# Three Strassen pairs in block 1 of an attention-and-GEGLU kernel, with the attention work of the next batches moved round them

## The chip, the cores and the metric

The kernel runs on one core of a Trainium2 chip. A core has a matrix engine (TensorE, PE in the profile), a vector engine (VectorE, DVE), an engine for activation functions (ScalarE, ACT), a general engine (GpSimd, POOL) and one that issues transfers (SyncE, SP). Each works through its own list of instructions in order, and they wait for each other by semaphores. The metric is the time of one execution in microseconds (us).

## The reference

Linear attention over 8 batches of 8 heads, 576 rows and 64 columns, and behind it a feed-forward layer with a GELU gate on the 4608 rows of 512 columns:

```python
q_s = exp(q - max(q)); q_s = q_s / sum(q_s, axis=-1)      # each row of q
k_s = exp(k - max(k)); k_s = k_s / sum(k_s, axis=2)       # each column of k
kv  = einsum('bhsd,bhse->bhde', k_s, v)
x   = einsum('bhsd,bhde->bhse', q_s, kv)                  # then (4608, 512)
g   = x @ w_gate                                          # 512 -> 1536
out = ((0.5 * g * (1 + erf(g / sqrt(2)))) * (x @ w_val)) @ w_out   # 1536 -> 512
```

## The kernel before

The rows are worked in blocks of 512, one for each batch (0 to 7), and one block (8) for the 64 rows of each batch that are left over. The order is 0 to 6, 8, 7. A block has a first stage (gate and value, twelve tiles of 128 columns, written to `ht`) and a second (the product with `w_out`). While PE works on block b, the other engines prepare batch b+1 and b+2 (exp, normalization, casts, transposes).

A direct tile takes four matmuls of 512 columns for the gate and four for the value. A pair takes two tiles k and k+3 together by a Winograd form of Strassen's method, on quarters: seven products of four matmuls of 256 columns, with sums of x (`xs`) and of the weights (`ws`) made ahead:

```python
def ffn_fi(xt, fi, spare=False):                  # a direct tile
    psg = bank([P, 512], "psg", not spare)
    mm_gv(psg, wg_sb, xt, fi, range(HP))
    psv = bank([P, 512], "psv", not spare)
    mm_gv(psv, wv_sb, xt, fi, range(HP))
    gate(psg, psv, fi)                            # gelu on ACT, product on DVE

def sum_x(xt, xs=xs):                             # four sums on GpSimd
    b11, b12, b21, b22 = (xt[:, c:c + 2, r:r + 256] for c in (0, 2) for r in (0, 256))
    ...
        nc.gpsimd.tensor_tensor(out=o, in0=a, in1=b, op=ALU.subtract)

def pair_step(b, xt, k, i):
    ...
    if i == 1:                                    # products 1 and 5; 5 reads xs[0]
        ...
    if i == 2:                                    # products 6 and 3
        ...
    elif i == 3:                                  # products 7 and 2, then upper(): a product
        ...                                       #   on GpSimd for the right half of h
    else:
        product_gv(4, pa, xt, k, False)           # and final(): gelu on ACT, product on DVE
```

The lists say in what order a block goes: `6g` and `6v` are the halves of direct tile 6, `0.1` is step 1 of pair 0, letters are places where other work rides along. Blocks 0 and 1 have no list: they take direct tiles.

```python
THREE = ("a 6g l 6v 0.1 9g 0.2 9v w 0.3 7g 0.4 n m 1.1 t 7v 1.2 10g 1.3 s0 10v 1.4 2.1 u0 8g 2.2 8v"
         " 2.3 s1 11g u1 2.4 11v x")
FOUR = ...
SIX = ("0.1 6.1 0.2 6.2 0.3 6.3 0.4 1.1 6.4 7.1 s0 1.2 7.2 1.3 u0 7.3 1.4 2.1 7.4 8.1 2.2"
       " 8.2 2.3 s1 8.3 2.4 u1")
steps = {b: (SIX if b >= B - 1 else THREE if b == 2 else FOUR).split() for b in range(2, B + 1)}
```

The second stage is seven products too (`psa`, `psb`, `psc` are its banks), with sums of h (`sum_h`: sh[1], sh[2], s4 and one in place). Sums of the last tiles come here:

```python
        get("b")
        product(1, ps["a"], False, js=js[4:])
        if b > 1 and not last:
            s1 = snap("a", True)                  # True: on ACT
        ride(b, PR, "e")
        sum_h(*last_js(b), (1, 2))
        if b < 2 or last:
            s1 = snap("a")
        product(2, ps["b"], True, js=js)
        add("b", s1, 0, 0)
        ...
        sum_h(*last_js(b), (4,), "pool" if b > 1 else "dve")
        get("c")
        product(5, ps["c"], True, js=js)
        sum_h(*last_js(b), (3,), "pool" if b > 1 else "dve")
        s5 = snap("c", b == B or b == B - 2)
        ride(b, NS, 1)
        product(6, ps["a"], False, js=js)
        s2 = snap("a", b == B or b == B - 2)
        ride(b, NS, 2)
        ...
        product(3, ps["c"], False, js=js[:cut])
        ...
        add("c", s2, 0, 1)
        ...
        store_rows(b, 0, yo[0])                   # SyncE
        ...
        if cut == NO:
            product(7, ps["a"], False, js=js)
            add("a", s5, 1, 1)
        ride(b, NS, 4)
        ...
        product(4, ps["a"], False, js=js)
```

What rides along in block 1, with v of every batch loaded to one buffer and cast to one (`ld_b["v"]`, `v16_b`):

```python
at(1, FI, 4, L(exp, "k", 2, 0, 4), L(norm, 2, 3, "pool"), L(sum_w, 4), make_s)
at(1, FI, 5, L(cast_v, 2, 0, H))
at(1, FI, 8, L(unit_td, 2))                       # DMA transpose of q
at(1, FI, 11, L(exp, "k", 2, 4, 8), L(exp, "q", 3))
at(1, NS, 2, L(unit_kv4, 2), L(exp, "k", 3), L(load_batch, 3, ((v, "v"),)), L(cast_v, 3, 0, H))
at(1, NS, 4, L(unit_x4, 2, ("act", "dve"), 1), one_ring, L(preload, ACTF.Gelu),
   lambda: sum_x(get_x(2)))
```

Of the kernel before, what the change touches and what calls it, by code (L numbers as in the profile page):

```python
# [9 lines left out]
f32 = mybir.dt.float32  # L10
f16 = mybir.dt.float16
ACTF = mybir.ActivationFunctionType
# [6 lines left out]
def kernel(  # L19
# [15 lines left out]
    P = 128  # L35
# [60 lines left out]
    def bank(shape, name, spare):  # L96
        return big(shape, f32, name) if spare else small(shape, f32, name)
# [375 lines left out]
        nc.vector.scalar_tensor_tensor(  # L473
            out=ht[:, fi, :], in0=psv, scalar=_H_SCALE, in1=gl, op0=ALU.mult, op1=ALU.mult)

    def ffn_fi(xt, fi, spare=False):
        psg = bank([P, 512], "psg", not spare)
        mm_gv(psg, wg_sb, xt, fi, range(HP))
        psv = bank([P, 512], "psv", not spare)
        mm_gv(psv, wv_sb, xt, fi, range(HP))  # L480
        gate(psg, psv, fi)

    def ffn_first(xt, after):

        ps = []
        for fi in range(len(after)):
            psg = big([P, 512], f32, "psg")
            psv = big([P, 512], f32, "psv")
            if fi == 0:
                for ci in range(2):  # L490
                    mm_gv(psg, wg_sb, xt, fi, [ci])
                    mm_gv(psv, wv_sb, xt, fi, [ci])
            else:
                mm_gv(psg, wg_sb, xt, fi, range(0, 2))
                mm_gv(psv, wv_sb, xt, fi, range(0, 2))
            ps.append((psg, psv))
            for f in after[fi]:
                f()
        for fi, (psg, psv) in enumerate(ps):
            mm_gv(psg, wg_sb, xt, fi, [2])  # L500
            mm_gv(psv, wv_sb, xt, fi, [2])
        for fi, (psg, psv) in enumerate(ps):
            mm_gv(psg, wg_sb, xt, fi, [3])
            mm_gv(psv, wv_sb, xt, fi, [3])
            gate(psg, psv, fi)
# [57 lines left out]
        for i in (1, 2):  # L563
            sh[i] = wstp.tile([P, NO, 256], f16, name=f"sh{i}", tag="wst")

    def sum_h(j0, j1, which, eng="dve"):
        step = 1 if j1 - j0 == 2 else NO // 2
        js, ks = slice(j0, j1, step), slice(NO + j0, NO + j1, step)
        a11, a21 = ht[:, js, 0:256], ht[:, js, 256:512]
        a12, a22 = ht[:, ks, 0:256], ht[:, ks, 256:512]  # L570
        s1, s2 = sh[1][:, js], sh[2][:, js]
        for i in which:
            o, a, b, op = {1: (s1, a21, a22, ALU.add), 2: (s2, s1, a11, ALU.subtract),
                           3: (a21, a11, a21, ALU.subtract),
                           4: (s4[:, js], a12, s2, ALU.subtract)}[i]
            (nc.gpsimd if eng == "pool" else nc.vector).tensor_tensor(out=o, in0=a, in1=b, op=op)  # L576
# [12 lines left out]
    def sum_x(xt, xs=xs):  # L589
        b11, b12, b21, b22 = (xt[:, c:c + 2, r:r + 256] for c in (0, 2) for r in (0, 256))  # L590
        t = [xs[:, i] for i in range(4)]
        for o, a, b in ((t[0], b12, b11), (t[1], b22, t[0]), (t[2], b22, b12), (t[3], b21, t[1])):
            nc.gpsimd.tensor_tensor(out=o, in0=a, in1=b, op=ALU.subtract)

    def product_gv(i, ps, xt, k, first):
# [3 lines left out]
        for t, w, nm in ((0, wv_sb, "v"), (1, wg_sb, "g")):  # L599
            ss = ws[(nm, k // NO)]  # L600
            for c in range(2):
# [6 lines left out]

    THREE = ("a 6g l 6v 0.1 9g 0.2 9v w 0.3 7g 0.4 n m 1.1 t 7v 1.2 10g 1.3 s0 10v 1.4 2.1 u0 8g 2.2 8v"
             " 2.3 s1 11g u1 2.4 11v x")
    FOUR = ("a 7g l 7v n 0.1 6.1 0.2 6.2 0.3 6.3 m 10g 0.4 6.4 1.1 t 10v 1.2 s0 8g u0 1.3 8v 1.4 2.1"
            " 11g s1 2.2 11v 2.3")
    SIX = ("0.1 6.1 0.2 6.2 0.3 6.3 0.4 1.1 6.4 7.1 s0 1.2 7.2 1.3 u0 7.3 1.4 2.1 7.4 8.1 2.2"
           " 8.2 2.3 s1 8.3 2.4 u1")
    steps = {b: (SIX if b >= B - 1 else THREE if b == 2 else FOUR).split() for b in range(2, B + 1)}
    live = {}

    def half(b, xt, c, nm):  # L620
# [9 lines left out]
    def pair_step(b, xt, k, i):  # L630
# [24 lines left out]
                op=ALU.mult)  # L655

        if i == 1:
            live["odd"] = odd = b > 2 and not live.get("odd", True)
            cc = cc_b if odd else ffn.tile([P, 2, 2, 256], f32, name="cc", tag="cc", bufs=1)
            pa = big([P, 2, 256], f32, "pga", True)  # L660
            product_gv(1, pa, xt, k, True)
            pb = big([P, 2, 256], f32, "pgb", True, True)
            nc.scalar.copy(out=pb, in_=pa)  # L663
            pc = big([P, 2, 256], f32, "pgc", True)
            product_gv(5, pc, xt, k, True)
            live[k] = [cc, pa, pb, pc, snap(pc, b >= B - 1)]
            return
# [35 lines left out]
            if late:  # L703
                late()

    SUMS = {7: (0, 2, (1, 2)), 8: (0, 2, (3, 4)), 9: (2, 4, (1, 2)), 10: (2, 4, (3, 4))}

    def product(i, ps, first, ts=(0, 1), js=range(NO)):
        for j in js:
            for t in ts:  # L710
# [10 lines left out]

    def get_x(b):
        return get_xt(b) if b < B else xtr

    def last_js(b):
        return (NO - 2 if b < 2 else NO // 2 - 1, NO)

    def out_strassen(b, last):
        yo = [yop.tile([P, 2, C], f32, name="yo", tag="yo") for _ in range(2)]
# [27 lines left out]
                    out=yo[half][:, t, c[col]], in0=src, scalar=1.0 / _H_SCALE,  # L757
                    in1=sn[:, t], op0=ALU.mult, op1=ALU.add)

        js = (0, 1, 2, 3, 4, 5) if b < 2 else (0, 3, 1, 4, 2, 5)  # L760
        get("a")
        four = 2 < b < B - 1
        cut = 3 if four else 4
        product(1, ps["a"], True, js=js[:cut])
        if four:
# [6 lines left out]
            pair_step(b, get_x(b), NFI - NO // 2 - 1, 4)  # L772
        get("b")
        product(1, ps["a"], False, js=js[4:])
        if b > 1 and not last:
            s1 = snap("a", True)
        ride(b, PR, "e")
        sum_h(*last_js(b), (1, 2))
        if b < 2 or last:
            s1 = snap("a")  # L780
        product(2, ps["b"], True, js=js)
        add("b", s1, 0, 0)
        for x in tiles_["b"]:
            let_go(x)
        sum_h(*last_js(b), (4,), "pool" if b > 1 else "dve")
        get("c")
        product(5, ps["c"], True, js=js)
        sum_h(*last_js(b), (3,), "pool" if b > 1 else "dve")
        s5 = snap("c", b == B or b == B - 2)
        ride(b, NS, 1)  # L790
        product(6, ps["a"], False, js=js)
# [12 lines left out]
        if last:  # L804
            finish_last(b, ps["a"], yo[1], s5)
            return
        if cut == NO:
            product(7, ps["a"], False, js=js)
            add("a", s5, 1, 1)
# [108 lines left out]
    def at(b, kind, i, *fns):  # L918
        plan.setdefault((b, kind, i), []).extend(fns)
# [3 lines left out]
    def load_2nd():  # L923
# [11 lines left out]
    at(0, NS, 7, L(exp, "q", 2))  # L935
    first1 = [[L(unit_t, 1, 1), L(unit_kv, 1, 1)],
              [L(unit_x, 1, 2, "dve"), L(preload, ACTF.Gelu)],
              [L(unit_x, 1, 3, "dve"), L(norm, 2, 0, "pool"), L(norm, 2, 1, "pool")]]

    def x_upper0():  # L940
        unit_x(0, 2, "act")
# [2 lines left out]
        kv0_norm(3)  # L944


    at(1, FI, 2, L(unit_trem, 1))
    at(1, FI, 3, L(norm, 2, 2, "pool"), L(load_batch, 3, ((q, "q"), (k, "k"))))
    at(1, FI, 4, L(exp, "k", 2, 0, 4), L(norm, 2, 3, "pool"), L(sum_w, 4), make_s)
    at(1, FI, 5, L(cast_v, 2, 0, H))  # L950
    at(1, FI, 8, L(unit_td, 2))
    at(1, FI, 11, L(exp, "k", 2, 4, 8), L(exp, "q", 3))
    at(1, NS, 2, L(unit_kv4, 2), L(exp, "k", 3), L(load_batch, 3, ((v, "v"),)), L(cast_v, 3, 0, H))
    at(1, NS, 4, L(unit_x4, 2, ("act", "dve"), 1), one_ring, L(preload, ACTF.Gelu),
       lambda: sum_x(get_x(2)))
    load_2 = lambda n: load_batch(n, ((v, "v"), (q, "q"), (k, "k")))
    for i, x in enumerate(("g1", "v1", "g2", "v2", "g4", "v4")):
        at(0, FI, 5 + i, L(sum_wgv, x[0], int(x[1])))
    at(0, FI, NFI - 2, L(sum_w, 1))
    at(1, NS, 2, L(sum_wgv, "g", 3), L(sum_wgv, "v", 3))  # L960
    for b in range(2, B):
        n = b + 1
        if n < B:
# [17 lines left out]
            at(b, NS, 4, L(preload, ACTF.Gelu))  # L981
        at(b, NS, 4, L(lambda n: sum_x(get_x(n)), n if n < B - 1 else B))
    at(B, NS, 2, L(lambda: sum_x(get_x(B - 1), xs_b[1])))
    for b in range(2, B + 1):
        for j in range(NO // 2 - 1):
            at(b, PR, f"s{j}", L(sum_h, j, NO, (1,)), L(sum_h, j, NO, (3,), "pool"))
            at(b, PR, f"u{j}", L(sum_h, j, NO, (2,)), L(sum_h, j, NO, (4,), "pool"))
    for i, xs_ in (("w", ("g1", "v1", "g2", "v2")), ("x", ("g4", "v4", "g3", "v3"))):
        for x in xs_:
            at(2, PR, i, L(sum_wgv, x[0], int(x[1]), NO, 1, "pool"))  # L990
# [5 lines left out]
    def ride(b, kind, i):  # L996
        for fn in plan.get((b, kind, i), []):
            fn()

    for b in order:  # L1000
        xt = get_xt(b) if b < B else xtr
        fi0 = 0
        if b < 2:
            if b == 0:
                ffn_first0(xt, (x_upper0, L(unit_x, 0, 3, "dve")))
            else:
                ffn_first(xt, first1)
            fi0 = 2 if b == 0 else 3
            ride(b, FI, fi0 - 1)
        if b > 1:  # L1010
            go_on(b, xt)
        for fi in range(fi0, NFI if b < 2 else 0):
            ffn_fi(xt, fi, b == 1 and fi == 7)
            ride(b, FI, fi)
            if b > 0 and fi in SUMS:
                sum_h(*SUMS[fi])
        if b == 0:
            psys = []
            for ns in range(4):
                psys.append(big([P, C], f32, "psy"))  # L1020
                mm_out(psys[ns], ns, range(0, NFI // 2))
                ride(b, NS, ns)
            for ns in range(4):
                cut = 9 if ns == 2 else 7 if ns == 3 else NFI
                mm_out(psys[ns], ns, range(NFI // 2, cut))
                ride(b, NS, 14 + ns)
                mm_out(psys[ns], ns, range(cut, NFI))
                evac(b, ns, psys[ns], "act" if ns == 3 else "dve")
                ride(b, NS, 4 + ns)
        else:  # L1030
            out_strassen(b, b == order[-1])
# [30 lines left out]
```

The softmax here doesn't subtract the row's maximum and nothing guards it: scores larger than these inputs give would overflow.

## Time and profile before

| what | value |
|---|---|
| time, median of 3 runs | 296.51 us (296.48 to 296.78) |
| span of the profiled execution | 294.7 us |
| matmuls | 2449 |
| mean granted clock of PE | 0.999 |

The profile is of one execution. Its page gives the busy time of each engine and, in 40 slices of the span, the busy share in tenths. In the order of time a row has the start, the duration (of the merged instructions), the engine, the line of the kernel, the operation with output and inputs, the shape, the count, and in brackets the idle time before it with what ended it. Rows of waits give total, count and longest. Durations of matmuls overlap, so the cost of one is read from the distance of starts. Block 1 has its first stage from about 48.7 to 70.9 us and its second to 82.1; block 2 follows.

### The profile page before, as it was taken

The numbers are of one execution on the slowest core, as the hardware profiler recorded it, in microseconds if no ns is written. First come the engines' busy times: TensorE is split into PE (matmuls) and PEld (weight loads), VectorE is DVE, ScalarE is ACT, GpSimd is POOL, SyncE is SP. The second block draws the span as 40 slices with busy tenths as digits, with TensorE's granted clock in tenths as the row PEclk, the third lists the DMA queues.
The fourth block names the chain that finished last, engine by engine and source line by source line (L and its number), as shares of the span: only waits on it lengthen the run. The fifth ranks groups of instructions, "written<-read, shape, count | busy, mean of one in ns | idle before, by whom it ended". The sixth has DMA issues, their size and how long they took to land. (4 is left out here: it accounts for less than half of the span.)

```text
span 294.7 us, 6354 instructions
## 1 busy us (share of the span) xinstructions
PE 283.5 (96%) x2449; PEld 202.8 (69%) x2449; DVE 226.0 (77%) x409; ACT 194.4 (66%) x321; POOL 205.9 (70%) x191
## 2 busy tenths in 40 slices
PE   3999999999999999999999999999999999899984
PEld 1544445446767687779777877687768888788863
DVE  2855888878878769768977896787678789849992
ACT  4663367776776589768976898589863576447730
POOL 1558647870499699868887788779886555774480
PEclk9999999999999999999999999999999999999999
DMA  6999999998069605970499039803050200032003
GB/s 225 373 382 389 400 391 392 337 323 231 3 224 383 108 3 174 382 157 3 153 373 206 2 136 350 232 1 122 24 100 2 120 24 1 2 91 55 0 2 142
DMA packets 54622, 51.72 MB, mean 176 GB/s; under 512 B 18496, under 2 KB 50496, under 8 KB 54592
## 3 DMA queue, kind: packets, MB, share of 16 engines
q1 hardware_dynamic: 52864, 49.49, 52.9%
q10 hardware_dynamic: 1728, 1.84, 1.9%
q8 instruction: 19, 0.31, 0.4%
q14 instruction: 11, 0.09, 0.1%
HBM read 37.75 MB, written 9.44 MB: 160 GB/s over the span
## 5 line engine op out<-in xcount | busy, mean ns | idle before, releaser
L467 PE MATMUL psg<-xt,wg_sb 128*128 128x512 f16 x184 | 49.3, 379 | 0.0
L467 PE MATMUL psv<-xt,wv_sb 128*128 128x512 f16 x184 | 49.2, 379 | 0.0
L718 PEld LDWEIGHTS <-ht 128*128 128x128 f16 x384 | 36.4, 98 | 10.1 <-issue 2.7
L250 POOL TENSOR_TENSOR eq<-eq,rrq 128x640 f16<-128x640 f16 (+1 forms) x27 | 34.7, 1302 | 11.7 <-DVE rrq L242 7.8
L576 POOL TENSOR_TENSOR ht<-ht 128x512 f16<-128x512 f16 x21 | 26.7, 1270 | 6.1 <-DVE sh L576 6.1
L606 PEld LDWEIGHTS <-wv_sb 128*128 128x128 f16 x248 | 24.1, 98 | 9.4 <-issue 1.0
L653 POOL TENSOR_TENSOR ht<-eq 128x512 f16<-128x512 f32 x14 | 17.8, 1273 | 18.0 <-ACT eq L651 18.0
L467 PEld LDWEIGHTS <-wv_sb 128*128 128x128 f16 x184 | 17.9, 98 | 18.0 <-issue 0.5
L576 POOL TENSOR_TENSOR s<-ht,sh 128x512 f16<-128x512 f16 x21 | 24.7, 1176 | 6.9 <-DVE sh L576 6.9
L467 PEld LDWEIGHTS <-wg_sb 128*128 128x128 f16 x184 | 17.9, 98 | 16.5
L634 DVE SCALAR_TENSOR_TENSOR ht<-pga,glq 128x256 f16<-128x256 f32 x31 | 13.0, 421 | 20.6 <-ACT glq L633 20.5
L188 POOL CAST v<-vt 128x640 f16<-128x640 f32 x26 | 19.1, 776 | 12.8 <-PE pskv L343 11.3
L606 PEld LDWEIGHTS <-wg_sb 128*128 128x128 f16 x248 | 24.2, 98 | 2.8
L653 POOL TENSOR_TENSOR ht<-cc 128x512 f16<-128x512 f32 x15 | 19.1, 1274 | 8.6 <-ACT cc L651 8.5
L472 ACT ACTIVATE gl<-psg 128x512 f32<-128x512 f32 x24 | 13.8, 597 | 16.9 <-PE psg L467 15.8
L633 ACT ACTIVATE glq<-pgb 128x256 f32<-128x256 f32 x31 | 11.7, 378 | 18.7 <-PE pgb L606 10.9
L718 PE MATMUL psa<-tw,ht 128*128 128x256 f16 x192 | 23.4, 272 | 0.2 <-DVE yo L756 0.2
L212 ACT ACTIVATE ek<-kt 128x1280 f16<-128x1280 f32 (+1 forms) x11 | 19.1, 1748 | 5.7 <-DMA kt<-in_k_dram 4.2
L473 DVE SCALAR_TENSOR_TENSOR ht<-psv,gl 128x512 f16<-128x512 f32 x24 | 16.0, 686 | 8.6 <-PE psv L467 6.8
L663 ACT COPY pgb<-pga 128x512 f32<-128x512 f32 x31 | 18.0, 580 | 6.9 <-PE pga L606 6.6
L643 ACT ACTIVATE snq<-pga 128x512 f32<-128x512 f32 x31 | 18.5, 599 | 4.0 <-PE pga L606 3.7
L718 PEld LDWEIGHTS <-sh 128*128 128x128 f16 x192 | 18.6, 98 | 2.8 <-DVE sh L576 0.4
(172 smaller groups left out, 732.0 us busy)
## 6 DMA issues: line engine op xcount, KB each, us to landing
out_dram<-yo SPq DMA_DIRECT2D x15, 512.0 KB, 3.4
kt<-in_k_dram SPq DMA_DIRECT2D x7, 640.0 KB, 8.6
vt<-in_v_dram SPq DMA_DIRECT2D x7, 640.0 KB, 5.0
qt<-in_q_dram SPq DMA_DIRECT2D x7, 640.0 KB, 7.6
qt<-in_q_dram SPq DMA_DIRECT2D x8, 512.0 KB, 7.8
wost<-in_moe_w_out_dram SPq DMA_DIRECT2D x6, 512.0 KB, 7.9
kt<-in_k_dram SPq DMA_DIRECT2D x6, 512.0 KB, 9.7
vt<-in_v_dram SPq DMA_DIRECT2D x6, 512.0 KB, 5.7
```

Source lines behind the costliest of these rows:

```text
L188: nc.gpsimd.tensor_copy(out=dst, in_=src)
L212: nc.scalar.activation(out=dst[:, n0:NC, h0 * D:h1 * D].rearrange(o, d=D, **({"t": 2} if b >= QUAD else {})), in_=heads(tiles[(nm, b)], b, ...
L250: (nc.gpsimd if eng == "pool" else nc.vector).tensor_tensor(out=e, in0=e, in1=rrq.unsqueeze(-1).to_broadcast((P, n, 2, D)), op=ALU.mult)
L467: nc.tensor.matmul(ps, w[:, ci, fi * P:(fi + 1) * P], xt[:, ci, :], start=(ci == 0), stop=(ci == HP - 1))
L472: nc.scalar.activation(out=gl, in_=psg, func=ACTF.Gelu)
L473: nc.vector.scalar_tensor_tensor(out=ht[:, fi, :], in0=psv, scalar=_H_SCALE, in1=gl, op0=ALU.mult, op1=ALU.mult)
L576: (nc.gpsimd if eng == "pool" else nc.vector).tensor_tensor(out=o, in0=a, in1=b, op=op)
L606: nc.tensor.matmul(ps[:, t], a, x, start=(first and t == 0 and c == 0), stop=(c == 1), skip_group_check=True)
L643: nc.scalar.activation(out=sn, in_=ps, func=ACTF.Copy, scale=_H_SCALE)
L653: (nc.vector if k == NFI - NO // 2 - 1 else nc.gpsimd).tensor_tensor(out=ht[:, k:k + NO // 2 + 1:NO // 2, 256:512], in0=cc[:, :, 0], in1=c ...
L663: nc.scalar.copy(out=pb, in_=pa)
L718: nc.tensor.matmul(ps[t], a, w, start=(first and j == js[0] and (t == ts[0] or ps[t].tensor is not ps[ts[0]].tensor)), stop=(j == js[-1]), ...
```

## The change

Block 1 gets three pairs (tiles 0 to 5) behind its first direct tiles, which are now 6 to 8. Sums of x for it are made on GpSimd, and the third and fourth sums of weights move from the end of block 1 to block 0. All exps of k of batch 2 go to the end of block 1, with the cast of its v; kv of batch 2, the load of v of batch 3 and its cast go behind the third product of the second stage. All eight PSUM banks form one ring from the start of the pairs on. In blocks 8 and 7 sums of h move from GpSimd to VectorE and behind the first product of the second stage, and ScalarE makes the first snap. The aim is fewer matmul columns in block 1, and sums that stand in the way of less.

```diff
-    def ffn_first(xt, after):
+    def ffn_first(xt, f0, after):
...
+    ONE = ("l 9g 9v n 0.1 1.1 0.2 1.2 0.3 1.3 m 10g 0.4 w 1.4 t 2.1 10v s0 2.2 u0 11g s1 2.3 11v c")
...
-           " 8.2 2.3 s1 8.3 2.4 u1")
-    steps = {b: (SIX if b >= B - 1 else THREE if b == 2 else FOUR).split() for b in range(2, B + 1)}
+           " 8.2 2.3 s1 8.3 2.4")
+    steps = {b: (ONE if b == 1 else SIX if b >= B - 1 else THREE if b == 2 else FOUR).split()
+             for b in range(1, B + 1)}
...
-        js = (0, 1, 2, 3, 4, 5) if b < 2 else (0, 3, 1, 4, 2, 5)
+        js, late = (0, 3, 1, 4, 2, 5), NO // 2 - 1
         get("a")
-        four = 2 < b < B - 1
+        four = b != 2 and b < B - 1
...
-        if b > 1 and not last:
+        if b > 1:
             s1 = snap("a", True)
         ride(b, PR, "e")
-        sum_h(*last_js(b), (1, 2))
-        if b < 2 or last:
+        sum_h(late, NO, (1,))
+        if b >= B - 1:
+            ride(b, PR, "u1")
+        sum_h(late, NO, (2,))
+        if b < 2:
             s1 = snap("a")
...
-        sum_h(*last_js(b), (4,), "pool" if b > 1 else "dve")
+        if b > 1:
+            sum_h(late, NO, (4,), "pool")
+        else:
+            sum_h(0, NO, (4,), "dve", 1)
...
+        ride(b, NS, 3)
         if cut == NO:
             product(7, ps["a"], False, js=js)
...
-              [L(unit_x, 1, 3, "dve"), L(norm, 2, 0, "pool"), L(norm, 2, 1, "pool")]]
+              [L(unit_x, 1, 3, "dve"), lambda: sum_x(get_x(1)), L(norm_pair, 2, 0, 0, ("pool", "pool"))]]
...
-    at(1, FI, 4, L(exp, "k", 2, 0, 4), L(norm, 2, 3, "pool"), L(sum_w, 4), make_s)
-    at(1, FI, 5, L(cast_v, 2, 0, H))
-    at(1, FI, 8, L(unit_td, 2))
-    at(1, FI, 11, L(exp, "k", 2, 4, 8), L(exp, "q", 3))
-    at(1, NS, 2, L(unit_kv4, 2), L(exp, "k", 3), L(load_batch, 3, ((v, "v"),)), L(cast_v, 3, 0, H))
...
-    at(1, NS, 2, L(sum_wgv, "g", 3), L(sum_wgv, "v", 3))
+    for i, x in ((4, "g1"), (5, "v1"), (6, "g2"), (7, "v2"), (8, "g3"), (9, "v3"), (10, "g4"), (10, "v4")):
+        at(0, FI, i, L(sum_wgv, x[0], int(x[1])))
+    at(0, FI, 10, L(sum_w, 1))
...
+    at(1, PR, "m", L(norm_mul, 2, 2, "pool"), L(norm_mul, 2, 3, "pool"))
+    at(1, PR, "w", L(sum_w, 4), make_s)
+    at(1, PR, "c", L(cast_v, 2, 0, H))
+    at(1, PR, "t", L(unit_td, 2))
+    at(1, PR, "e", L(exp, "k", 2, 0, 4), L(exp, "k", 2, 4, 8), L(exp, "q", 3))
+    at(1, NS, 3, L(unit_kv4, 2), L(exp, "k", 3), L(load_batch, 3, ((v, "v"),)), L(cast_v, 3, 0, H))
+    at(1, NS, 4, L(unit_x4, 2, ("act", "dve"), 1), L(preload, ACTF.Gelu), lambda: sum_x(get_x(2)))
...
+            at(b, PR, f"s{j}", L(sum_h, j, NO, (1,)))
+            if j and b >= B - 1:
+                at(b, PR, f"u{j}", L(sum_h, j, NO, (2, 3, 4)))
+            else:
+                at(b, PR, f"s{j}", L(sum_h, j, NO, (3,), "pool"))
...
-                ffn_first(xt, first1)
-            fi0 = 2 if b == 0 else 3
+                ffn_first(xt, NO, first1)
+                one_ring()
...
-        if b > 1:
+        if b > 0:
             go_on(b, xt)
```

## The prediction

> **What bounds the kernel now.** I read the page's busy shares and slices first, then the waits of TensorE, then the order of time on TensorE, GpSimd, SyncE and VectorE round the stages that the change touches. The page:
>
> ```profile
> PE 283.5 (96%) x2449; PEld 202.8 (69%) x2449; DVE 226.0 (77%) x409; ACT 194.4 (66%) x321; POOL 205.9 (70%) x191
> PE   3999999999999999999999999999999999899984
> ```
>
> A busy PE is not a PE at its peak, so I asked what its matmuls waited for. The waits of PE in the whole span are these (total, times, longest):
>
> ```profile
> PE pswarm L459 <- ACT warm L861: 4.9, 1, 4.9
> PE psb L718 <- DVE ht L634: 1.8, 2, 0.9
> PE psx L418 <- DVE kv_sb L326: 0.3, 1, 0.3
> PE psa L718 <- DVE yo L756: 0.2, 1, 0.2
> PE psa L718 <- DVE sn L750: 0.2, 1, 0.2
> ```
>
> After the first load TensorE loses some 2.5 us. So time can be won in two ways only, fewer matmul columns or those last waits, and is lost wherever a new wait reaches PE. The price of both kinds of tile stands side by side in PE's order of time at the start of block 2:
>
> ```profile
> 82.91 1.03 PE L467 MATMUL psv<-xt,wv_sb 128*128 128x512 f16 x4
> 83.77 0.38 PE L606 MATMUL pga<-xt,wv_sb 128*128 128x256 f16 x2
> 83.99 0.38 PE L606 MATMUL pga<-xt,wg_sb 128*128 128x256 f16 x2
> 84.21 0.38 PE L606 MATMUL pgc<-xs,wsv 128*128 128x256 f16 x2
> ```
>
> By starts, four 512-column matmuls take 0.86 us and one product (four of 256) 0.44 us. The last line is the first reader of xs in block 2. GpSimd made it so, in its order of time:
>
> ```profile
> 62.66 2.71 POOL L188 CAST v<-vt 128x640 f16<-128x640 f32 x4
> 76.71 3.36 POOL L188 CAST v<-vt 128x640 f16<-128x640 f32 x4 [11.34 <-PE pskv L343]
> 81.69 1.15 POOL L593 TENSOR_TENSOR xs<-xt 128x512 f16<-128x512 f16 x1 [1.63 <-ACT xt L190]
> ```
>
> The reader is to see that the cast of v of batch 2 (62.66) and of batch 3 (76.71) lie well ahead, and that the sums xs stand behind the second cast on an engine that works in order. The load of batch 3 between them, on SyncE, and the landing of six v loads from 66.9 us on:
>
> ```profile
> 62.74 4.08 SPq L386 DMA_TRANSPOSE eqt<-eq  x1
> 66.92 1.29 SPq L168 DMA_DIRECT2D vt<-in_v_dram  x2
> 80.12 4.11 SPq L545 DMA_DIRECT2D out_dram<-yo  x2
> DMA to landing us min/median/max: 4.9/5.3/5.6
> ```
>
> **What the Trainium skill says.** "Perfetto Trace Analysis", section Identifying the Most-Contended Engine: matmul busy share says little of the distance to the peak, weight-load share more. The trace has 96% and 69%, which is why I went by starts. "DMA: Bandwidth & Descriptors", section Anatomy of one DMA: a semaphore wait is made on the issuing sequencer before dispatch. The trace agrees: SyncE stood 12.4 us before the store at 80.12, so nothing behind a store in its order can go earlier. "GPSIMD Engine Reference", section Key points: it shares its SBUF interfaces with VectorE when that has two SBUF inputs. The trace agrees: sums of h that take 0.42 us on VectorE took 1.25 to 1.38 beside GpSimd. "TensorE: Matmul & The Clock Gate", section What's actually happening: an idle window of about 3.4 us throttles the clock, and as much work frees it. Here the fifteen warm-up matmuls from 4.91 us took 6.25 us, 0.42 each, where later ones of the same 512 columns start every 0.22; no long gap follows in this trace, so it doesn't show a return to the slow clock.
>
> **The change part by part.**
>
> *Three pairs in block 1.* A pair replaces 16 matmuls of 512 (4 x 0.86 = 3.46 us) by 7 products (7 x 0.44 = 3.06). Three pairs: -1.2 us on PE. It needs sums of x (4 x 1.15 us on GpSimd). They follow the two sums tw, which ended at 55.3; so xs[0] is there at 56.5 and is read at 57.5. The third and fourth sums of weights move to block 0, where VectorE has about 1 us free per tile: nothing on the path.
>
> *The end of block 1.* Laid out with these durations from 55.4 us, PE comes to the last product of the third pair at about 70.4. Its gelu (0.38) and multiplication (0.42) end at 71.4, and the first product wants it at 70.8: a wait of 0.6. VectorE then has late sums (2 x 0.4), a snap (0.65), an addition (0.65), six sums s4 in one (0.9 to 1.6 beside casts) and a second snap (0.65). It frees the bank for product three between no and 0.7 us late. So product three ends at about 77.2. Before it ended at 78.3, but with kv of batch 2 (0.76 us of PE) ahead of it, which now comes behind: of the 1.2 won some 0.35 is left.
>
> *v of batches 2 and 3.* There is one v buffer. The cast of v 2 now stands at the end of the pairs, so it is done at about 75; the load of v 3 stands in SyncE's order behind the store of the first half of block 1's output. Added up: product three 77.2; bank read, addition of 0.69 with 0.15 to start: 78.0; issue of the store, about 1.0: 79.0; second v load issued 0.65 later: 79.7; landing 5.3: 85.0; four casts 3.0 (2.7 to 3.4 in the trace): 88.0; xs[0] 1.15: 89.2. In GpSimd's order of the changed kernel the casts of v 3 stand before the sums xs, as they did. The first reader of xs on PE stood at 84.2 before. So it is about 5.0 us later, though PE's own work (kv 0.77, product seven 1.31, x 0.9, product four 1.31, the first tile 1.73, one product 0.44, and 0.3 for a late copy of x) would have allowed 84.0: an idle PE of some 5.2 us. What the exp of k 3 behind the later kv costs (2.3 us of ScalarE, up to 0.4 of PE) vanishes inside this.
>
> *The clock.* A gap of 5 us is longer than the window named above. If it throttles, one window of 3.4 us (the skill's figure) runs at about half speed, an estimate of 1.7 us lost. I take it at two in three: +1.1. GpSimd's remaining lag of about 1.3 us against PE in block 2, against idle of 1.8 before its last upper product, I put at +0.2.
>
> *Blocks 8 and 7.* VectorE and PE at the end of block 8:
>
> ```profile
> 253.01 1.38 DVE L576 TENSOR_TENSOR sh<-sh,ht 128x512 f16<-128x512 f16 x1
> 254.31 0.41 DVE L634 SCALAR_TENSOR_TENSOR ht<-pga,glq 128x256 f16<-128x256 f32 x1
> ...
> 252.61 1.26 PE L718 MATMUL psb<-wo_sb,ht 128*128 128x256 f16 x10
> 254.77 0.39 PE L718 MATMUL psb<-wo_sb,ht 128*128 128x256 f16 x2 [0.91 <-DVE ht L634]
> ```
>
> A sum slowed by GpSimd to 1.38 us stands before the last h, which PE waits for. The change puts that sum behind it and takes two sums from GpSimd. The last h would then be done at 253.4, before PE's slot at 253.7. Product three started at 257.71, where three products of 1.31 from 252.61 give 256.54: 1.17 to be had, and in block 7 (281.40 to 286.83 against 3.93) 1.50. I count 2.4 of the 2.7.
>
> Sum: +5.0 (with what the pairs win already in it) + 1.1 + 0.2 - 2.4 = +3.9 on 296.5: 300.4 us.
>
> **Rivals.** *The late v is harmless*: 84.2 becomes 84.0, and the time falls by 0.2 + 2.4 to some 293.9; without the waits of block 1 to 293. For it speaks that the change moved kv back on purpose; against it each link of the chain is a duration of the trace, with 5 us to spare. *No throttling*: 299.3; the gap may fall across two windows. *The end of block 1 is worse than I laid out*: VectorE and ScalarE have seven products of three pairs almost back to back, and lateness there adds to product three and so to the whole chain, up to 2 us, 302.5. *The waits of blocks 8 and 7 only move*: ScalarE now takes all of the first snap of block 7, and the late sums still stand before product six; then 1 to 2 us more, 301.5 to 302.5. In block 3 the same layout runs without a PE wait, which speaks against the third.
>
> **Range and chances.** The chain's links sum to an uncertainty of about 1 us, the clock is 0 or 1.7, blocks 8 and 7 between -1 and -2.7, block 1's end up to +2. Eight in ten: 297.0 to 302.6. Slower by over 2% means 302.4, which needs two of these to go wrong together: 0.12. Faster by over 2% means 290.6, below the first rival: 0.01. Within: 0.87.
>
> **What would show it.** In the changed profile: a wait of some 5 us of PE pgc for POOL xs at the start of block 2, POOL waiting for the v load just before its casts, the v loads on SyncE directly after a store near 79; a granted clock below 1 after it; no wait of psb for ht in blocks 8 and 7. I am wrong if the casts of v 3 start before 80, or if PE waits in block 1 for longer than 1 us.

## The result, and the profile after

The changed kernel takes 304.47 us (median of four executions, 303.70 to 304.75), against 296.60 for the kernel before (296.48 to 296.78). The ratio is 1.026, with a 95% interval of 1.024 to 1.028: slower by 2.6%. The prediction, 300.4 with a range of 297.0 to 302.6, was too low. The execution that was profiled took 303.70 us; its span is 301.9, against 294.7 before.

First the page of the changed kernel. Busy times, then the slices of PE and of its clock:

```profile
PE 284.3 (94%) x2485; PEld 206.9 (69%) x2485; DVE 225.6 (75%) x409; ACT 197.2 (65%) x332; POOL 212.9 (71%) x197
PE   3999999997757999999999999999999999999994
PEclk9999999999997999999999999999999999999998
```

The total busy time hardly says that anything happened. The slices do: PE falls to 7, 7, 5 and 7 in slices 10 to 13, each 7.5 us long, so from some 68 to 98 us, and in the last of these the clock falls too. Between the first slice and the last everything else stands at 9. The waits of PE give the names (total, times, longest):

```profile
PE pgc L605 <- POOL xs L592: 5.4, 1, 5.4
PE pswarm L459 <- ACT warm L864: 4.9, 1, 4.9
PE psc L717 <- DVE sn L746: 1.7, 1, 1.7
PE pga L605 <- DVE cc L648: 1.0, 1, 1.0
PE psa L717 <- DVE ht L635: 0.5, 1, 0.5
```

The wait at the start (4.9) is as before; the two waits for `ht` of blocks 8 and 7 (1.8 in all) are gone. In their place stand one of 5.4 for the sums of x in block 2 and three of 3.2 together. PE's order of time shows that these three lie at the end of block 1 (start, duration, then in brackets the idle time before and what ended it):

```profile
71.06 0.38 PE L605 MATMUL pga<-xs,wv_sb 128*128 128x256 f16 x2 [1.03 <-DVE cc L648]
72.59 0.39 PE L717 MATMUL psa<-wo_sb,ht 128*128 128x256 f16 x2 [0.50 <-DVE ht L635]
...
78.89 1.47 PE L717 MATMUL psc<-wo_sb,s 128*128 128x256 f16 x12 [1.71 <-DVE sn L746]
80.29 0.82 PE L343 MATMUL pskv<-v,ek 128*64 128x65 f16 x40
...
92.46 0.58 PE L605 MATMUL pgc<-xs,wsv 128*128 128x256 f16 x2 [5.38 <-POOL xs L592]
93.26 1.91 PE L467 MATMUL psg<-xt,wg_sb 128*128 128x512 f16 x4
```

The first reader of `xs` in block 2, at 84.21 before, is at 92.46. Product three (the row at 78.89) gives way to the next work at 80.29, where the prediction had it end at 77.2. SyncE and GpSimd show the chain from there. SyncE's order of time:

```profile
81.12 0.59 SPq L545 DMA_DIRECT2D out_dram<-yo  x1
81.84 1.46 SPq L168 DMA_DIRECT2D vt<-in_v_dram  x2
```

GpSimd's:

```profile
73.01 3.29 POOL L188 CAST v<-vt 128x640 f16<-128x640 f32 x4
...
88.59 2.71 POOL L188 CAST v<-vt 128x640 f16<-128x640 f32 x4 [11.17 <-DMA vt<-in_v_dram]
91.26 1.15 POOL L592 TENSOR_TENSOR xs<-xt 128x512 f16<-128x512 f16 x1
```

The reader sees the load of v of batch 3 directly behind the store, and GpSimd idle for 11 us because that load has not landed, with the sums `xs` behind its casts. Behind the gap the clock is slow. A table by stage (length of the stretch, busy time of PE, PEld, DVE, ACT and POOL with counts, clock, DMA share, GB/s):

```profile
86.00:92.40 6.40, 1.08 (x7) 0.59 (x6) 1.59 (x3) 1.88 (x5) 3.81 (x5) 0.97 0.47 178
92.40:95.60 3.20, 3.14 (x12) 1.62 (x12) 0.00 (x0) 0.98 (x2) 3.12 (x4) 0.53 0.86 251
```

From 92.4 to 95.6 us PE had about half its clock (0.53): the four matmuls of 512 columns at 93.26 took 1.91 us, where they take 1.03. The work from 92.46 to 95.63 (eight matmuls of 256 columns and four of 512) costs 8 x 0.109 + 4 x 0.216 = 1.74 us by the usual starts, and took 3.17.

Blocks 8 and 7 did what they were meant to. PE at the end of block 8, products two and three, with five and six cut between them:

```profile
262.43 1.47 PE L717 MATMUL psb<-wo_sb,ht 128*128 128x256 f16 x12
...
266.36 1.47 PE L717 MATMUL psc<-wo_sb,s 128*128 128x256 f16 x12
```

No bracket, and three products of 1.31 from start to start: 3.93 us from product two to product three, where the kernel before took 5.10. Block 7 has 290.06 to 293.99, 3.93 for 5.43. Together 2.67 us won.

So the spans add up as follows: the first reader of `xs` 8.25 later (92.46 against 84.21), the slow clock 1.43, blocks 8 and 7 -2.67, the rest of blocks 2 to 6 +0.2: +7.2. The other three executions have spans of 302.7 to 303.0 at mean clocks of 0.987 and 0.988, against 0.992 in the profiled one. They are not traced; they fit a longer slow stretch, such as the trace of experiment 3 shows (last section).

### The profile page after: what moved, and what is told of

Its sections match the earlier page's. It is cut to its first block, busy times and chain, and to the rows that moved or that the text cites. A ratio compares the mean times of both kernels' runs of the same rounds, so it can differ in the third digit from the quotient of the medians.

```text
span 301.9 us, 6439 instructions
## 1 busy us (share of the span) xinstructions
PE 284.3 (94%) x2485; PEld 206.9 (69%) x2485; DVE 225.6 (75%) x409; ACT 197.2 (65%) x332; POOL 212.9 (71%) x197
## 4 chain that ended last, share of the span: by engine, by line
PE 69%; DMA 2%; DVE 1%; POOL 1%; issue 0%; SPq 0%; POOLq 0%
PE pga L605 18%; PE psa L717 13%; PE pgc L605 9%; PE psc L717 7%; PE psg L467 6%; PE psv L467 6%; PE pgb L605 4%; PE psb L717 3%; DMA vt<-in_v_dram 2%; PE pskv L343 2%; PE psx L430 1%; POOL v L188 1%; DVE s L575 1%; POOL xs L592 0%; PE psxr L430 0%
## 5 line engine op out<-in xcount | busy, mean ns | idle before, releaser
L467 PE MATMUL psg<-xt,wg_sb 128*128 128x512 f16 x160 | 44.2, 386 | 0.0
L467 PE MATMUL psv<-xt,wv_sb 128*128 128x512 f16 x160 | 43.1, 379 | 0.0
L635 DVE SCALAR_TENSOR_TENSOR ht<-pga,glq 128x256 f16<-128x256 f32 x34 | 14.4, 422 | 22.2 <-ACT glq L634 22.1
L575 POOL TENSOR_TENSOR s<-ht,sh 128x512 f16<-128x512 f16 x19 | 22.4, 1177 | 9.9 <-DVE sh L575 9.9
L654 POOL TENSOR_TENSOR ht<-cc 128x512 f16<-128x512 f32 x17 | 21.9, 1291 | 9.3 <-ACT cc L652 9.3
L664 ACT COPY pgb<-pga 128x512 f32<-128x512 f32 x34 | 19.8, 582 | 7.3 <-PE pga L605 7.0
L240 DVE TENSOR_REDUCE rq<-eq 128x20 f32<-128x1280 f16 (+1 forms) x14 | 20.1, 1439 | 4.6 <-ACT eq L212 4.6
L644 ACT ACTIVATE snq<-pga 128x512 f32<-128x512 f32 x34 | 20.3, 600 | 4.4 <-PE pga L605 4.1
L605 PE MATMUL pga<-xs,wv_sb 128*128 128x256 f16 x112 | 21.4, 272 | 1.0 <-DVE cc L648 1.0
L605 PE MATMUL pga<-xs,wg_sb 128*128 128x256 f16 x112 | 21.4, 273 | 0.0
```

Of the source, the lines that this page charges most:

```text
L240: nc.vector.reduce_sum(rq, e, axis=mybir.AxisListType.X)
L467: nc.tensor.matmul(ps, w[:, ci, fi * P:(fi + 1) * P], xt[:, ci, :], start=(ci == 0), stop=(ci == HP - 1))
L605: nc.tensor.matmul(ps[:, t], a, x, start=(first and t == 0 and c == 0), stop=(c == 1), skip_group_check=True)
L635: nc.vector.scalar_tensor_tensor(out=ht[:, fi, 0:256], in0=ps[:, 0], scalar=_H_SCALE, in1=gl, op0=ALU.mult, op1=ALU.mult)
L644: nc.scalar.activation(out=sn, in_=ps, func=ACTF.Copy, scale=_H_SCALE)
L654: (nc.vector if k == NFI - NO // 2 - 1 else nc.gpsimd).tensor_tensor(out=ht[:, k:k + NO // 2 + 1:NO // 2, 256:512], in0=cc[:, :, 0], in1=c ...
```

## Experiments

The theory after the result had three parts. (1) The 5.4 us of waiting come from SyncE: the load of v of batch 3 stands behind a store that waits for product three. (2) Product three is late because VectorE's sums of h are two to three times as long as laid out, beside a GpSimd that never rests. (3) The rest of the change is small, and blocks 8 and 7 are worth what they were meant to be. (A bank is one of the eight PSUM buffers that matmuls write to. A snap is the scaled copy that frees one.) Rivals: the wait for `xs` would come with any late v, whoever stands ahead of it; VectorE simply has too many instructions there; and the gain of blocks 8 and 7 depends on the state in which block 1 leaves the engines.

**Experiment 1: the load ahead of the store.** One line of the changed kernel; the load is issued behind product six, before the store comes up in SyncE's order.

```diff
-    at(1, NS, 3, L(unit_kv4, 2), L(exp, "k", 3), L(load_batch, 3, ((v, "v"),)), L(cast_v, 3, 0, H))
+    at(1, NS, 2, L(load_batch, 3, ((v, "v"),)))
+    at(1, NS, 3, L(unit_kv4, 2), L(exp, "k", 3), L(cast_v, 3, 0, H))
```

> The changed kernel with one edit: the load of v of batch 3 is issued behind the sixth product (ahead of the store of the first half of block 1's output on SyncE), its cast and kv of batch 2 stay behind the third. Theory (the load stands behind the store and so holds up the casts, the sums xs and PE): the load can go when the cast of v 2 is done (77 us), lands at about 83, xs[0] at about 86.5; the wait of PE for xs falls from 5.4 to under 1 us, the clock stays at 1.0 in block 2, the time falls by 5.4 + 1.4 to about 297.7 us. Rival (GpSimd is late for another reason, the casts waiting for kv of batch 2 or its own backlog): xs is hardly earlier and the time stays within 1.5 us of 304.5.

Measured: 296.68 us, ratio to the kernel before 1.0007 (0.9999 to 1.0016), mean clock 0.999. SyncE in this kernel:

```profile
76.35 1.29 SPq L168 DMA_DIRECT2D vt<-in_v_dram  x2
81.14 6.42 SPq L545 DMA_DIRECT2D out_dram<-yo  x2
```

GpSimd:

```profile
82.69 2.71 POOL L188 CAST v<-vt 128x640 f16<-128x640 f32 x4 [5.25 <-PE psa L717]
85.36 1.15 POOL L592 TENSOR_TENSOR xs<-xt 128x512 f16<-128x512 f16 x1
```

The store goes at the same time as in the changed kernel; the load goes 5.5 us earlier, `xs` stands 5.9 us earlier, and PE reads it at 86.93 without a wait. The three waits in block 1 stay as they were (1.7, 1.0, 0.5). So the place of one load in SyncE's order is worth 304.47 - 296.68 = 7.8 us here: the wait, and the clock behind it. This settles part 1 against its rival. It also leaves a bill: this kernel has the gain of blocks 8 and 7 and is still no faster than the kernel before.

**Experiment 2: blocks 8 and 7 alone.** The kernel before, with only the part of the diff that concerns its last two blocks (cut to its core):

```diff
-        if b > 1 and not last:
+        if b > 1:
             s1 = snap("a", True)
...
-        sum_h(*last_js(b), (1, 2))
-        if b < 2 or last:
+        sum_h(*last_js(b), (1,))
+        if b >= B - 1:
+            ride(b, PR, "u1")
+        sum_h(*last_js(b), (2,))
+        if b < 2:
             s1 = snap("a")
...
+            if j and b >= B - 1:
+                at(b, PR, f"u{j}", L(sum_h, j, NO, (2, 3, 4)))
```

> The kernel before with the change in blocks 8 and 7 alone. Theory (the waits of psb for h and of the sums behind them were 2.6 us, and go): 294.0 us, both waits of psb gone. Rival (the waits move to product six or three of these blocks, and the 2.6 us that block 2's end to the end of the kernel won in the changed kernel came from other blocks): 295.5 to 296.6 us.

Measured: 293.91 us, ratio 0.991 (0.989 to 0.993). After the start PE waits once, for 0.2 us. The kernel before took 296.52 beside it, so the part gives 2.6 us without anything done to block 1, and doesn't depend on it. Then the rest of the change, with the load already repaired, costs 296.68 - 293.91 = 2.8 us. The first readers of `xs` say the same: 86.93 against 84.22, 2.7 us. That is block 1 with its three waits.

**Experiment 3: GpSimd quiet at the end of block 1.** The changed kernel without two lines of work for GpSimd. It leaves out the cast of v of batch 2 and half the normalization of its q, so it does less than it should and its time is read only for what happens in block 1. VectorE's list is the same.

```diff
-    at(1, PR, "m", L(norm_mul, 2, 2, "pool"), L(norm_mul, 2, 3, "pool"))
...
-    at(1, PR, "c", L(cast_v, 2, 0, H))
```

> The changed kernel without two pieces of GpSimd's work in block 1: the multiplication of q of batch 2 by its reciprocal sums for head pairs 2 and 3, and the cast of v of batch 2 (left out, so batch 2 is worked with old values there). Theory (VectorE's sums at the end of block 1 are slow because GpSimd works beside them): the sums of h, 0.55 to 1.37 us each in the changed kernel, take 0.4 to 0.5, the six in one about 1.0 instead of 1.88, and PE's waits in block 1 (1.0, 0.5 and 1.7 us) fall to under 1 in total. Rival (VectorE is late because what it waits for comes late, and the durations are those of the instructions themselves): durations and waits stay.

Measured, one execution: 301.5 us. VectorE's order of time in the changed kernel, rows of sums of h and snaps:

```profile
69.03 1.37 DVE L575 TENSOR_TENSOR sh<-ht 128x512 f16<-128x512 f16 x1
70.32 0.68 DVE L648 SCALAR_TENSOR_TENSOR cc<-pga,snq 128x512 f32<-128x512 f32 x1
...
76.36 1.88 DVE L575 TENSOR_TENSOR s<-ht,sh 128x1536 f16<-128x1536 f16 x1
78.16 0.68 DVE L746 TENSOR_SCALAR sn<-psc 128x512 f32<-128x512 f32 x1
```

and the same rows with GpSimd quiet:

```profile
69.04 0.41 DVE L575 TENSOR_TENSOR sh<-ht 128x512 f16<-128x512 f16 x1
69.38 0.68 DVE L648 SCALAR_TENSOR_TENSOR cc<-pga,snq 128x512 f32<-128x512 f32 x1
...
74.50 0.95 DVE L575 TENSOR_TENSOR s<-ht,sh 128x1536 f16<-128x1536 f16 x1
75.36 0.69 DVE L746 TENSOR_SCALAR sn<-psc 128x512 f32<-128x512 f32 x1
```

The rows are those that PE's waits name. At 69.03 one sum takes 1.37 instead of 0.41, the addition `cc` behind it starts 0.94 later, and PE's wait of 1.03 for `cc` is there; without the slow sum it isn't. The six sums in one (`s`) take 1.88 instead of 0.95, and with three earlier sums (0.90, 0.93 and 0.82, against 0.91, 0.41 and 0.42) the snap of `psc` starts at 78.16 instead of 75.36. The rows that read PSUM (`cc`, the snaps) take 0.68 or 0.69 in both. The table of the window from 64 to 78 us has, for the changed kernel,

```profile
64.00:78.00 14.00, 11.54 (x90) 8.40 (x87) 13.01 (x18) 10.39 (x14) 12.89 (x12) 1.00 0.33 74
```

and with those instructions left out:

```profile
64.00:78.00 14.00, 13.31 (x132) 10.09 (x132) 12.05 (x21) 10.47 (x14) 6.50 (x6) 1.00 0.41 80
```

GpSimd is busy for 12.89 of 14 us in one and 6.50 in the other (2.66 in the kernel before), while the transfers are the same, 74 and 80 GB/s. So it isn't the DMA that slows the sums. Product three starts at 76.10 instead of 78.89 and kv at 77.50 instead of 80.29: 2.8 of the 3.1 us by which the prediction's 77.2 was missed.

How late a sum is depends on what GpSimd is doing when its turn comes. GpSimd's rows in the changed kernel beside the sums of 69.03 and 76.36:

```profile
68.79 1.33 POOL L575 TENSOR_TENSOR ht<-ht 128x512 f16<-128x512 f16 x1
...
76.27 1.15 POOL L575 TENSOR_TENSOR ht<-ht 128x512 f16<-128x512 f16 x1
```

The sum of 69.03 ends at 70.40, 0.28 us after GpSimd's instruction (70.12). The sums of 68.23 and 72.45 end 0.28 and 0.29 after the GpSimd instruction that runs when they begin (69.11 for 68.83, 73.35 for 73.06), and the six in one 0.82 after theirs (78.24 for 77.42). So in these rows a sum that begins beside a GpSimd instruction is through only when that has ended, and is late by what was left of it. The kernel before shows the same at the end of block 3, the layout that the prediction trusted. The sums of 129.29, 134.05 and 134.38 begin in pauses of GpSimd and take 0.41 to 0.42. The next one doesn't (VectorE's row, then GpSimd's), and ends 0.28 after GpSimd:

```profile
134.83 1.26 DVE L576 TENSOR_TENSOR sh<-sh,ht 128x512 f16<-128x512 f16 x1
...
134.54 1.27 POOL L576 TENSOR_TENSOR s<-ht,sh 128x512 f16<-128x512 f16 x1 [0.64 <-DVE sh L576]
```

The Trainium skill, "GPSIMD Engine Reference", section Key points, names this contention for VectorE instructions with two SBUF inputs, without a size; here sums of 0.41 us took 0.55 to 1.37, and what reads PSUM was not slowed. The rival "too many instructions" falls, as VectorE has the same ones. The wait for `xs` stays, 5.0 us, for the order on SyncE is unchanged.

**Experiment 4: the load ahead, and less on VectorE.** Experiment 1, with the sums of weights `tw` (1.27 us) moved out of the pairs to behind product six, and block 1's first snap on ScalarE:

```diff
-        if b > 1:
+        if b > 0:
             s1 = snap("a", True)
...
-    at(1, PR, "w", L(sum_w, 4), make_s)
+    at(1, PR, "w", make_s)
+    at(1, NS, 2, L(sum_w, 4))
```

> The load ahead as in the first, and VectorE relieved at the end of block 1: the fourth sum of w_out (1.27 us) goes behind the sixth product, and the first snap of block 1 goes to ScalarE (0.68 us). Theory (VectorE's order is what PE waits for in block 1): the waits of 1.0 and 1.7 us fall to under 1 in total, the time to about 295 us. Rival (GpSimd's last upper product, not VectorE's own work, sets it): the waits stay near 2 us, 297 us or more.

Measured: 297.1 us (20 executions; the profiled one 298.2), ratio 1.003 (1.002 to 1.004). A miss: no gain over experiment 1. The executions fall into two groups, eleven from 296.63 to 297.15, as long as experiment 1, and nine from 297.82 to 298.38; the median lies at the edge between them, and the trace is of the longer group. In this trace the waits of block 1 did shrink, from 3.2 us to 1.1, and product three starts 2.5 us earlier, at 76.36. But a new wait of 3.3 us for `xs` took it all. GpSimd:

```profile
72.19 4.09 POOL L188 CAST v<-vt 128x640 f16<-128x640 f32 x4
...
83.92 2.71 POOL L188 CAST v<-vt 128x640 f16<-128x640 f32 x4 [6.51 <-DMA vt<-in_v_dram]
```

The cast of v of batch 2 began earlier but took 4.09 us, and frees the one load buffer at 76.3, as in experiment 1. The load goes at 76.31, its second half needs up to 6.8 us to land (5.5 in experiment 1), and PE, which could have read `xs` at 84.5, stands until 87.8. The store now goes at 78.85, while the load is on its way; that this is what slows the load is likely, but not shown. The chain through v had been hidden behind the waits of block 1, with hardly any room to spare. The clock did not fall behind this gap of 3.3 us:

```profile
87.80:91.20 3.40, 3.40 (x24) 2.28 (x24) 0.79 (x2) 1.68 (x3) 3.38 (x4) 1.00 0.86 271
```

**Experiment 5: the cast off GpSimd's path.** Experiment 4, with the cast of v of batch 3 on ScalarE, in two halves inside block 2 (places `y` and `z`), and the load of v of batch 4 behind the second half (the diff is against the changed kernel):

```diff
-    at(1, NS, 3, L(unit_kv4, 2), L(exp, "k", 3), L(load_batch, 3, ((v, "v"),)), L(cast_v, 3, 0, H))
+    at(1, NS, 2, L(load_batch, 3, ((v, "v"),)))
+    at(1, NS, 3, L(unit_kv4, 2), L(exp, "k", 3))
+    at(2, PR, "y", L(cast_v, 3, 0, 4, "act"))
+    at(2, PR, "z", L(cast_v, 3, 4, 8, "act"), L(load_batch, 4, ((v, "v"),)))
```

> The version with the load ahead and VectorE relieved, and the cast of v of batch 3 taken off GpSimd: ScalarE makes it in two halves in the idle places of block 2 (1.6 us each before the change), the load of v of batch 4 follows the second. Theory (what held xs in the version before it, 3.3 us, was the casts standing ahead of the sums on GpSimd while they waited for the load): the wait for xs goes to 0, so do the waits for cc in block 2, the time is 297.1 - 3.3 - 0.4 = about 293.4 us. Rival (ScalarE's casts push gelus and copies back in block 2): PE waits 1 us or more in block 2, 294.5 or more.

Measured: 294.22 us, ratio 0.992 (0.991 to 0.994). The sums `xs` follow x directly, at 82.72, and PE reads them at 84.63 without a wait. The direction is right. The time is 0.8 us above the 293.4 expected, but that sum took waits of one trace off a median that stands for other executions too: taken off the execution that was traced (298.2), 3.3 and 0.4 leave 294.5. Block 1 still has 0.5 + 0.3 + 0.3 of waits.

**Experiment 6: and another order of the last pair.** Experiment 5, with the direct tile 11 between the steps of pair 2, so that VectorE's work for the pair has time, and the pair's last product ahead of that tile's value half, no longer inside product one of the second stage (`four`):

```diff
-    ONE = ("... 2.1 10v s0 2.2 u0 11g s1 2.3 11v c")
+    ONE = ("... 2.1 10v s0 2.2 u0 2.3 s1 11g u1 2.4 11v c")
...
-        four = b != 2 and b < B - 1
+        four = 2 < b < B - 1
```

> As the fifth, and block 1 ends like block 2: the last product of the third pair goes ahead of the value half of tile 11 instead of into the first product of the second stage, and the second group of sums of h goes behind the third step of the last pair. Theory (the waits of 0.3 for cc and 0.5 for h come from a gelu and a multiplication with too little PE work behind them): both go, and the 0.3 us for sn falls: 0.8 less than the fifth, about 292.7 us, which would be 1.2 below the change of blocks 8 and 7 alone. Rival (VectorE's sums beside GpSimd set it in any order): within 0.3 us of the fifth.

Measured: 293.73 us, ratio 0.991 (0.989 to 0.992). After the start PE has one line of waits left:

```profile
PE pga L605 <- ACT snq L644: 0.2, 1, 0.2
```

Block 1 runs nearly without a wait, and yet the time is 1 us above what was expected. The comparison is with the kernel with blocks 8 and 7 alone (experiment 8), counted in each trace from the start of block 1 (48.45 here, 48.78 there). The second stage begins 0.49 us earlier than there (70.14 and 70.96), not 1.2: two pauses among the pairs, of 0.41 us behind 66.18 (with the wait of 0.2) and 0.30 behind 67.68, took the rest. Product four begins 0.55 earlier, and the reader of `xs` only 0.13. PE's order of time has the last loss:

```profile
79.92 1.49 PE L717 MATMUL psa<-tw,ht 128*128 128x256 f16 x12
81.39 1.29 PE L467 MATMUL psg<-xt,wg_sb 128*128 128x512 f16 x4
82.52 1.03 PE L467 MATMUL psv<-xt,wv_sb 128*128 128x512 f16 x4
...
83.82 0.38 PE L605 MATMUL pgc<-xs,wsv 128*128 128x256 f16 x2
```

and in experiment 8:

```profile
80.80 1.47 PE L718 MATMUL psa<-tw,ht 128*128 128x256 f16 x12 [0.22 <-DVE yo L756]
...
84.28 0.38 PE L606 MATMUL pgc<-xs,wsv 128*128 128x256 f16 x2
```

Between the two the first tile of block 2 starts late (1.47 us behind product four, 1.31 in experiment 8), and its gate half takes 1.13 from start to start, not 0.87. ScalarE's order of time in experiment 6 has the reason:

```profile
73.56 2.44 ACT L212 ACTIVATE ek<-kt 128x1280 f16<-128x1280 f32 x2
75.90 2.32 ACT L212 ACTIVATE eq<-qt 128x2560 f16<-128x2560 f32 x1
78.12 2.32 ACT L212 ACTIVATE ek<-kt 128x2560 f16<-128x2560 f32 x1
80.35 0.51 ACT L190 CAST xtr<-psxr 128x128 f16<-128x128 f32 x2
```

With the change the exps stand there in a row without a break: both halves of k of batch 2, q of batch 3 and k of batch 3 (before the change the first half of k stood earlier in block 1). In the kernel of experiment 8 the last of them comes after 1.5 us of rest:

```profile
77.20 2.34 ACT L212 ACTIVATE ek<-kt 128x2560 f16<-128x2560 f32 x1 [1.50 <-issue]
```

Here it begins at 78.12, and the copies of x wait for its end at 80.35, though PE began x at 79.17. This is read from the trace; no run moved the exps.

**Experiment 7: the sums of weights behind kv.** Experiment 6, with `tw` moved once more, behind kv, as it stood 0.3 us in x's way on VectorE:

```diff
-    at(1, NS, 2, L(sum_w, 4))
...
-    at(1, NS, 3, L(unit_kv4, 2), L(exp, "k", 3))
+    at(1, NS, 3, L(unit_kv4, 2), L(sum_w, 4), L(exp, "k", 3))
```

> The sixth with one sum moved: the fourth sum of w_out goes behind kv of batch 2 on VectorE. In the sixth it took 1.78 us there beside GpSimd and stood ahead of kv, and PE began the x of batch 2 0.3 us late. Theory (that gap of 0.3 us is kv waiting behind this sum, and pairs of block 1 pay once the queues behind them are free): the gap goes, about 293.4 us, 0.3 to 0.6 below the change of blocks 8 and 7 alone. Rival (block 1's pairs win nothing over direct tiles however they are fed): equal to blocks 8 and 7 alone within 0.2 us.

Measured: 293.75 us, ratio 0.991 (0.989 to 0.992). A miss: PE begins x 1.41 us behind product seven, as in experiment 8, instead of 1.57, and the time stayed. The copies of x on ScalarE stand directly behind the last exp again, at 80.57, which is 31.90 us after the start of block 1 (48.67), exactly as in experiment 6.

**Experiment 8: blocks 8 and 7 alone, beside experiment 7 on one chip.** The kernel of experiment 2 again, so that the two candidates are compared directly.

> The kernel before with the change of blocks 8 and 7 alone, once more beside the seventh on one chip: 293.9 us as before under either theory.

Measured: 293.89 us (293.75 to 294.05), ratio 0.991 (0.990 to 0.993), against 293.75 (293.65 to 293.79) for experiment 7. The difference of 0.14 us lies inside the intervals of both. So the three pairs in block 1, as well as these runs could feed them, bring nothing that can be measured here. Whether they would with the exps out of the way stays open. The kernel to keep is the one before with the change of blocks 8 and 7 alone: 2.5 us beside 296.42 here, 2.6 in experiment 2, 0.9%, for a few moved lines.

## Why the prediction was wrong

By its own steps:

- **Three pairs in block 1: -1.2 on PE.** Right as a count. By its own work PE comes to the last product of the third pair at 70.03 (71.06 less the wait of 1.03), where the prediction had 70.4. What the pairs win isn't kept, though: experiments 7 and 8 put what is left of it at 0.14 us even with the waits of block 1 gone.
- **The end of block 1: product three ends at 77.2.** This is the step that failed. It laid out VectorE's late sums at 0.4 each and the six sums at 0.9 to 1.6, and allowed a bank up to 0.7 us late. Measured: sums of 0.55 to 1.37, the six sums 1.88, waits of 1.03 for `cc` and 1.71 for the bank, and product three over at 80.3, 3.1 us later. The wait for the last h had the right size (0.50 for 0.6), in part by luck: PE came to the third pair's last product 0.37 earlier than laid out, and used the last h 1.53 us after its start (71.06 to 72.59), where the layout has 1.0 (70.4 to 71.4). The layout also counts two sums behind the last h; the trace has three (0.90, 0.93, 0.82). The prediction had the mechanism in its hands: it cites GpSimd's contention with VectorE and the 1.25 to 1.38 us of such sums, then lays out block 1 with the undisturbed 0.4, although the change moves GpSimd's work into this very window (12.9 of 14 us busy, 2.7 before). Its third rival, "the end of block 1 is worse than I laid out", is what happened, at 3.1 instead of "up to 2 us". It was set aside because block 3 runs the same layout without a wait of PE; what GpSimd does there was not weighed, and in the kernel before most of those sums begin in its pauses (experiment 3).
- **v of batches 2 and 3.** Right, each link to within some 0.6 us, from the wrong start. Predicted from the end of product three to `xs[0]`: 77.2 to 89.2, 12.0 us. Measured: 80.3 to 92.4, 12.1 (store issued at 81.12, loads at 81.84, casts at 88.59, `xs` at 91.26 for 1.15). PE's own work without the wait ends at 87.08 in the trace; the prediction's 84.0 with the 3.1 added is 87.1. The idle PE was 5.4 for 5.2. A late product three moves both ends of this wait, so the gap keeps its size and the whole goes to the end of the kernel.
- **The clock: 1.7, at two in three.** Right in kind. The profiled execution lost 1.43 us, 0.3 more than the expectation of 1.1 that went into the sum; the other three are 0.8 to 1.1 us longer still, which fits the rival that "the gap may fall across two windows": experiment 3, with their mean clock (0.988), lost 2.40 (last section).
- **GpSimd's lag in block 2: +0.2.** The rest between the slow clock and block 3 is 0.12.
- **Blocks 8 and 7: -2.4.** Right: -2.67 in the trace, 2.6 us by experiment 2. The fourth rival, that their waits only move, fell.

The sum of the prediction with the measured terms put in: +5.0 + 3.1 from the failed step, + 1.4 for the clock, + 0.1 for the rest, - 2.7, is +6.9 of the 7.2 us by which the spans differ. The median of the time is 0.8 us higher than the profiled execution.

## What to carry to other kernels

A load inherits the waits of whatever stands ahead of it on the engine that issues it, so place it by what frees its buffer, ahead of a store that waits for results; here one line was worth 7.8 us. When a change packs work onto GpSimd, ask of each of VectorE's two-input sums in that window what GpSimd is doing at its turn, and lay it out with the disturbed duration from the trace, not with the quiet one. And test parts of a change alone: the part that paid here was the smallest, and the one that the change was named for brought nothing once its own waits and those that took their place were counted.

## What the runs showed that was not expected

The length of a gap alone doesn't say what the clock costs. Read in steps of 0.1 us, the granted clock of the changed kernel was at half from 92.0 to 95.4 us. In experiment 3 it fell inside the gap already, at 87.5, and stayed at half to 94.3 (same columns as the tables above):

```profile
84.00:89.00 5.00, 0.29 (x3) 0.10 (x2) 0.83 (x2) 1.10 (x3) 3.53 (x5) 0.85 0.40 155
89.00:93.00 4.00, 3.66 (x14) 1.95 (x14) 0.00 (x0) 1.25 (x3) 3.92 (x5) 0.50 0.82 244
```

That is 3.4 us and 6.8 us, twice as long, with a gap that was shorter (5.0 against 5.4). PE's work from 89.34 to 94.78 there costs 12 x 0.109 + 8 x 0.216 = 3.04 us by the usual starts and took 5.44: 2.40 lost, against 1.43. In the trace of experiment 4 a gap of 3.3 us left the clock at 1.00, but three of its other executions have a mean clock of 0.992 or 0.993, so that is no safe limit. This fits the window of about 3.4 us that the Trainium skill names in "TensorE: Matmul & The Clock Gate", section What's actually happening; three gaps don't prove its length.

GpSimd slows in its turn beside VectorE: the same four casts of v took 2.71 us in block 2, where VectorE has little to do, and 3.29 to 4.09 beside VectorE's sums at the end of block 1.
